# Storing only the rows that are needed, with an earlier band matrix and earlier transposes, in a convolution and spectral-mixing kernel

## The chip, the cores and the metric

The kernel runs on one core of one Trainium2 chip. The metric is device microseconds (us) of one execution. Most executions of one kernel agree within a few tenths of a per cent up to one per cent (the four fast ones of e17 took 190.2 to 190.98 us); a few fall into a slower state (193.1 and 194.22 us of e17) and are left out of the ratios. The experiments ran in four calls. Each call ran on one chip, together with runs of the kernel before, and the calls were on different chips; so a ratio holds within its call, and times of different calls compare less sharply.

## The reference

A causal convolution of 7 taps along the sequence, whose taps are softmax-normalised for each of 8 heads, then a spectral layer: the first 64 frequencies of the sequence are mixed over the 192 channels by complex matrices, transformed back and added, and a ReLU branch with a 192 x 192 matrix follows.

```python
batch, seq, d_model = (8, 3264, 192)        # n_heads 8, kernel_size 7, n_modes 64
w = softmax(weight, axis=-1)                # per head
x[b, s] = sum_k w[h, k] * x_pad[b, s + k]   # 6 zero rows ahead of the sequence
X = np.fft.rfft(x, axis=1)
Yr = Xr @ w_r - Xi @ w_i                    # for each of 64 modes, 192 x 192
Yi = Xr @ w_i + Xi @ w_r
y = np.fft.irfft(Y, n=S, axis=1)            # the other modes are zero
u = x + y
return u + np.maximum(u @ w_ch, 0.0)        # (8, 3264, 192), float32
```

## The kernel before

The sequence is cut into 27 windows of 122 rows (`WIN`), each held in the 128 partitions of the on-chip memory with 6 rows of overlap. The kernel first loads x and applies the convolution as a band matrix (`conv_unit`) and the forward transform. Then it streams 16 groups of mixing weights, and applies them one group at a time (`mix`). In the shadow of these mixes TensorE transposes the convolved x (`t_next`, one "pair" of chunks per call), because the last phase needs it that way. The last phase makes the output: 27 windows x 2 halves of the batch x 2 = 108 units, each ending in one VectorE add (of the sums in PSUM, where the kernel's matmuls leave them, and of x); two units fill one tile `t` of 128 partitions x 4 images x 192 values, and one store sends it off.

The stores and their order:

```python
    def finish_unit(u, zp):
        ...
        add = nc.vector.tensor_tensor(out=t[:, 2 * k:2 * k + 2, :], in0=zp[...], in1=x_all[...], op=ALU.add)
        if k == 0:
            return
        if w == NWIN - 1:
            rows = ((0, 80), (80, LASTVALID))
        elif w % CH == CH - 1:
            rows = ((0, 112), (112, WIN))
        else:
            rows = ((0, P),)                # 128 rows: 6 wrong ones, put right by the next window's store
        for i, (r0, r1) in enumerate(rows):
            dst = bass.AP(tensor=out.tensor, offset=out.offset + (4 * h * S + WIN * w + r0) * D,
                          ap=[[D, r1 - r0], [S * D, B // 2], [1, D]])
            if i == 0:
                nc.sync.dma_start(out=dst, in_=t[r0:r1, :, :])
            else:
                rest.append((dst, t[r0:r1, :, :]))   # six small rests, issued by ScalarE at the very end

    CH = 9                                  # chains of nine windows, three side by side
    wq = [(h, st + CH * c) for st in range(CH) for c in range(3) for h in range(2)]
```

A window has 122 good rows, but 128 are stored. The six too many lie where the next window's first rows belong, so the next window's store has to come after this one: a chain. Three chains per half run side by side, so that no store waits: in the profile of the kernel before, SyncE's queue waits ahead of its stores for adds (51.1 us) and for weights, never for an earlier store.

The mixes and the transposes in their shadow:

```python
    for g in range(NGRP):                   # 16 groups
        ...
        m = mix(g)
        ...
        if g in (0, 1, 2):
            load_weights(g + 7, wp)
        elif 7 <= g and g + 3 < NGRP:
            load_weights(g + 3, wp)         # the load of group 10 needs the buffer of group 7
        if not last:
            for _ in range(1 if g < 7 else 2):
                t_next(2 if g < 6 else 3)
            ...
        mix_t(g, *m)
```

In the last phase TensorE works with two row tiles of 64 rows each (64\*128 on the page, where the convolution has 128\*128). A tiny instruction, here called a word, by another engine orders the two tiles where both write the same sums; before, GpSimd gives it (`word = nc.gpsimd.nop()`, 17 ns each in the trace).

## Time and profile before

| | before |
|---|---|
| median of the first runs | 193.16 us (193.13 to 196.17) |
| span in the profile | 191.2 us |
| first convolution matmul | 17.87 us |
| x landed | 61.94 us |
| mix 0 / mix 7 starts | 75.41 / 89.81 us |
| last weights landed | 112.63 us |
| first / fifth add starts | 120.01 / 122.35 us |
| last add ends / last store landed | 181.56 / 189.83 us |
| store packets of 768 B, mean / median / 90th percentile | 40 / 38 / 44 ns |

The table is read from the trace. One row of one image is 192 x 4 = 768 B and is one packet (the stores of SyncE are 27,008 packets of 768 B in the trace). The prediction below shows the views that carry it. This is the list of transfer issues on the page of the kernel before, with the kilobytes of each and the median us from issue to landing, and it shows that SyncE's stores are nearly all of one kind, 384 KB, which is 128 rows of 4 images (SPq is SyncE's queue):

```profile
out_dram<-t SPq DMA_DIRECT2D x48, 384.0 KB, 5.1
```

Windows of the kernel before: start:end, length, busy time and count of PE, PEld, DVE, ACT, POOL, granted clock, DMA share, GB/s. PE is TensorE, PEld its loading of weights, DVE VectorE, ACT ScalarE, POOL GpSimd and SP SyncE. The granted clock is the share of TensorE's full clock that it was given. The DMA share is the time that all packets took, over the time of the core's 16 DMA engines (which carry out the transfers); it can exceed 1.

```profile
4.00:6.00 2.00, 0.00 (x0) 0.00 (x0) 1.93 (x3) 0.00 (x0) 2.00 (x2) 1.00 0.77 73
6.00:8.00 2.00, 0.00 (x0) 0.00 (x0) 1.92 (x5) 0.25 (x1) 2.00 (x3) 1.00 1.60 191
8.00:10.00 2.00, 0.00 (x0) 0.00 (x0) 1.84 (x6) 0.85 (x3) 2.00 (x3) 1.00 1.59 188
```

### The profile page before, as it was taken

The numbers are of one execution on the slowest core, as the hardware profiler recorded it, in microseconds if no ns is written. First come the engines' busy times: TensorE is split into PE (matmuls) and PEld (weight loads), VectorE is DVE, ScalarE is ACT, GpSimd is POOL, SyncE is SP. The second block draws the span as 40 slices with busy tenths as digits, with TensorE's granted clock in tenths as the row PEclk, the third lists the DMA queues.
The fourth block names the chain that finished last, engine by engine and source line by source line (L and its number), as shares of the span: only waits on it lengthen the run. The fifth ranks groups of instructions, "written<-read, shape, count | busy, mean of one in ns | idle before, by whom it ended". The sixth has DMA issues, their size and how long they took to land.

```text
span 191.2 us, 5496 instructions
## 1 busy us (share of the span) xinstructions
PE 152.2 (80%) x2146; PEld 131.1 (69%) x2146; DVE 128.5 (67%) x251; ACT 120.5 (63%) x217; POOL 49.5 (26%) x76
## 2 busy tenths in 40 slices
PE   0046657988997996999898889999999999999700
PEld 0002336777986874888686767999999999999500
DVE  7995742635334344466967735899999999999900
ACT  2196694454572662576686636888888888888500
POOL 8994334332523941520453100000000000000000
PEclk9999955899999998799999999999999999999985
DMA  1999999999999999999899920499999999999995
GB/s 18 171 191 191 192 192 192 192 193 192 194 191 193 194 202 208 206 206 184 122 194 196 202 38 2 141 318 318 323 324 318 322 322 322 319 326 324 309 276 157
DMA packets 65450, 41.47 MB, mean 217 GB/s; under 512 B 29968, under 2 KB 65424, under 8 KB 65424
## 3 DMA queue, kind: packets, MB, share of 16 engines
q0 software_dynamic: 37088, 20.14, 76.9%
q1 hardware_dynamic: 28016, 20.77, 35.6%
q8 instruction: 17, 0.28, 0.5%
q10 hardware_dynamic: 320, 0.20, 0.5%
q14 instruction: 9, 0.07, 0.1%
HBM read 40.31 MB, written 20.94 MB: 320 GB/s over the span
## 4 chain that ended last, share of the span: by engine, by line
DMA 35%; PE 28%; DVE 22%; POOL 6%; issue 2%; ACT 1%; DVEq 0%; POOLq 0%; ACTq 0%
DMA x_all<-in_x_dram 26%; DVE t L503 17%; PE z L451 9%; DMA wt<-in_moe_w_r_dram 9%; PE tp L361 7%; PE z L469 6%; POOL x_all L61 4%; PE yp L394 3%; DVE tail L322 2%; DVE cTa L365 2%; PE zwps L417 1%; PE z L441 1%; PE yp L404 1%; DVE cTb L365 1%; POOL wt L225 1%
## 5 line engine op out<-in xcount | busy, mean ns | idle before, releaser
L503 DVE TENSOR_TENSOR t<-z,x_all 128x384 f32<-128x384 f32 x108 | 59.8, 557 | 3.7 <-PE z L469 1.9
L474 ACT ACTIVATE z<-z 128x384 f32<-128x384 f32 x108 | 51.0, 475 | 10.5 <-ACT z L474 0.3
L469 PE MATMUL z<-zw,gst 64*128 64x384 bf16 x216 | 47.2, 323 | 0.2
L451 PE MATMUL z<-zw,gst 64*128 64x384 bf16 x216 | 46.7, 323 | 0.0
L451 PE MATMUL z<-win,cTa 64*128 64x192 bf16 x390 | 44.4, 243 | 0.0
L244 ACT CAST x_all<-cp 122x768 bf16<-122x768 f32 (+2 forms) x32 | 26.9, 878 | 22.7 <-PE cp L237 22.7
L451 PEld LDWEIGHTS <-cTa 64*128 64x128 bf16 x468 | 36.7, 94 | 1.8
L237 PE MATMUL cp<-x_all,cband 128*128 128x240 bf16 (+2 forms) x192 | 26.5, 279 | 8.4 <-DVE x_all L232 3.2
L246 DVE CAST x_all<-cp 122x960 bf16<-122x960 f32 (+2 forms) x16 | 17.0, 1063 | 21.5 <-PE cp L237 21.4
L237 PEld LDWEIGHTS <-cband 128*128 128x128 bf16 x192 | 18.8, 105 | 14.9 <-issue 8.4
L61 POOL DMA_DIRECT2D x_all<-in_x_dram x24 | 23.7, 1002 | 18.3 <-DMA x_all<-in_x_dram 18.3
L257 PE MATMUL xp<-x_all,fst 122*128 122x192 bf16 (+1 forms) x216 | 22.9, 255 | 0.9 <-DVE x_all L246 0.5
L257 PEld LDWEIGHTS <-fst 122*128 122x128 bf16 (+1 forms) x216 | 18.9, 102 | 2.2 <-DVE x_all L246 0.7
L451 PEld LDWEIGHTS <-gst 64*128 64x128 bf16 x216 | 19.9, 94 | 0.7 <-issue 0.2
L367 ACT COPY cTa<-tp 128x854 bf16<-128x854 bf16 (+1 forms) x16 | 14.5, 909 | 8.1 <-PE tp L361 8.1
L469 PEld LDWEIGHTS <-gst 64*128 64x128 bf16 x216 | 18.7, 94 | 1.0 <-POOLq L486 0.9
L451 PE MATMUL z<-win,cTb 64*128 64x192 bf16 x130 | 19.1, 243 | 0.0
L451 PE MATMUL z<-wB,cTa 64*128 64x192 bf16 x78 | 18.9, 243 | 0.0
L225 POOL DMA_DIRECT2D wt<-in_moe_w_r_dram x16 | 9.9, 618 | 28.3 <-PE yp L394 22.8
L365 DVE COPY cTa<-tp 128x854 bf16<-128x854 bf16 (+1 forms) x17 | 10.6, 625 | 8.5 <-PE tp L361 8.3
L176 PE MATMUL bps<-scaled,ident 128*128 128x512 bf16 x7 | 4.1, 585 | 14.0 <-ACT scaled L174 14.0
L361 PE MATMUL tp<-ident,x_all 122*128 122x122 bf16 x216 | 15.0, 224 | 0.0
(90 smaller groups left out, 181.4 us busy)
## 6 DMA issues: line engine op xcount, KB each, us to landing
out_dram<-t SPq DMA_DIRECT2D x48, 384.0 KB, 5.1
wt<-in_moe_w_r_dram POOLq DMA_DIRECT2D x16, 288.0 KB, 6.4
wt<-in_moe_w_i_dram POOLq DMA_DIRECT2D x16, 288.0 KB, 7.4
x_all<-in_x_dram POOLq DMA_DIRECT2D x8, 432.0 KB, 16.5
x_all<-in_x_dram POOLq DMA_DIRECT2D x9, 384.0 KB, 17.8
x_all<-in_x_dram POOLq DMA_DIRECT2D x7, 480.0 KB, 18.4
out_dram<-t SPq DMA_DIRECT2D x4, 336.0 KB
out_dram<-t SPq DMA_DIRECT2D x2, 240.0 KB, 4.4
```

Source lines behind the costliest of these rows:

```text
L61: nc.gpsimd.dma_start(out=x_all[:, b, c0:c0 + n, :], in_=src)
L237: nc.tensor.matmul(cp[:, j, 0:GRP * n].rearrange("p (w e) -> p w e", w=n), cband[:, h, :], x_all[:, b, w0:w0 + n, GRP * h:GRP * h + GRP], ...
L244: nc.scalar.copy(out=dst, in_=srcv)
L246: nc.vector.tensor_copy(out=dst, in_=srcv)
L257: nc.tensor.matmul(xp[:, 0:D], fst[0:k, c, :], x_all[0:k, b, c, :], start=(c == 0), stop=(c == NWIN - 1))
L361: nc.tensor.transpose(tp[:, WIN * k:WIN * k + WIN], slot_lhsT(p, k0 + k), ident[0:WIN, 0:WIN])
L365: nc.vector.tensor_copy(out=dst, in_=tp[:, 0:WIN * n])
L367: nc.scalar.copy(out=dst, in_=tp[:, 0:WIN * n])
L451: return nc.tensor.matmul(o, lhsT, rhs, start=start, stop=stop, skip_group_check=True, tile_position=(lo, 0))
L469: return [lambda: nc.tensor.matmul(zp[:, 0:2 * D], gst[lo:hi, WIN * w:WIN * w + P], zwi[(h, 1, k)][lo:hi, :], start=False, stop=(r == 1), ...
L474: return nc.scalar.activation(out=zp[:, 0:2 * D], in_=zp[:, 0:2 * D], func=ACT.Relu)
L503: add = nc.vector.tensor_tensor(out=t[:, 2 * k:2 * k + 2, :], in0=zp[:, 0:2 * D].rearrange("p (i e) -> p i e", i=2), in1=x_all[:, 4 * h + ...
```

## The change

The intent was to shorten both transfer phases. Stores send exactly the 122 good rows, as 112 rows by SyncE and 10 by GpSimd, so no bytes are sent twice, no chains are needed and no rests are left for the end. The band matrix is built packed (8 heads x 38 columns), so that the convolution starts earlier. The transposes are brought forward (two pairs in each of the first eight mixes). The first four units run on the whole array. ScalarE gives the words instead of GpSimd. The first large load is issued ahead of other setup work.

```diff
-        if w == NWIN - 1:
-            rows = ((0, 80), (80, LASTVALID))
-        elif w % CH == CH - 1:
-            rows = ((0, 112), (112, WIN))
-        else:
-            rows = ((0, P),)
-        for i, (r0, r1) in enumerate(rows):
-            dst = ...
-            if i == 0:
-                nc.sync.dma_start(out=dst, in_=t[r0:r1, :, :])
-            else:
-                rest.append((dst, t[r0:r1, :, :]))
+        r1, r2 = (80, LASTVALID) if w == NWIN - 1 else (112, WIN)
+        for q, ra, rb in ((nc.sync, 0, r1), (nc.gpsimd, r1, r2)):
+            dst = bass.AP(tensor=out.tensor, offset=out.offset + (4 * h * S + WIN * w + ra) * D,
+                          ap=[[D, rb - ra], [S * D, B // 2], [1, D]])
+            q.dma_start(out=dst, in_=t[ra:rb, :, :])
-    CH = 9
-    wq = [(h, st + CH * c) for st in range(CH) for c in range(3) for h in range(2)]
+    wq = [(0, worder[0])]                    # windows in their natural order, the halves one apart
+    for i in range(1, NWIN):
+        wq.append((0, worder[i]))
+        wq.append((1, worder[i - 1]))
+    wq.append((1, worder[-1]))
@@ transposes
-            for _ in range(1 if g < 7 else 2):
+            for _ in range(2 if g < 8 else 1):
@@ words of order
-                    word = nc.gpsimd.nop()
+        word = nc.scalar.nop()               # and one word a step instead of two
@@ band matrix: 28 ScalarE scalings and 7 predicated copies become
+        nc.vector.scalar_tensor_tensor(out=scaled[:, k, :, :], in0=diagc[...], scalar=float(k),
+                                       in1=wsb[...], op0=ALU.is_equal, op1=ALU.mult)   # 7 times
+        for o in bps:
+            nc.tensor.matmul(o[:, 0:H * NB], ident[:], scaled[...], start=(k == 0), stop=(k == KK - 1))
@@ first units
+    zw_part(0, 0, "va"); zw_part(0, 1, "vv")
+    for n in range(2): g_full(seq[n], zps[n], 0); relu(zps[n])     # whole array, no row tiles
+    ...
@@ cut: order of the loads, sine tables by unit, evictions, end of the rests
```

## The prediction

> **What bounds the kernel now.** I read the 40 slices first, then the windows, then who waited for whom, then the issuing queues. The slices:
>
> ```profile
> PE   0046657988997996999898889999999999999700
> PEld 0002336777986874888686767999999999999500
> DVE  7995742635334344466967735899999999999900
> ...
> DMA  1999999999999999999899920499999999999995
> GB/s 18 171 191 191 192 192 192 192 193 192 194 191 193 194 202 208 206 206 184 122 194 196 202 38 2 141 318 318 323 324 318 322 322 322 319 326 324 309 276 157
> ```
>
> A slice is 4.78 us. There are two transfer phases, with a hole between them. From about 5 to 111 us the load queue runs at 191 to 208 GB/s (x, then 16 groups of expert weights); from 122 to 189 us the stores run at about 320. So three things can shorten the program: an earlier or denser load phase, a smaller hole, a shorter store phase. The work of the engines inside a full transfer phase counts only through these. The windows show where each phase is loose:
>
> ```profile
> 86.00:90.00 4.00, 3.73 (x77) 3.16 (x78) 2.77 (x8) 2.48 (x5) 0.00 (x0) 1.00 1.20 205
> 90.00:91.00 1.00, 1.00 (x26) 0.91 (x23) 0.29 (x3) 1.00 (x2) 0.34 (x1) 1.00 0.44 73
> 91.00:92.00 1.00, 0.99 (x19) 0.87 (x17) 0.92 (x2) 0.71 (x2) 0.87 (x2) 1.00 0.22 22
> 92.00:93.00 1.00, 1.00 (x24) 0.80 (x22) 1.00 (x4) 0.95 (x3) 0.00 (x0) 1.00 0.68 46
> 93.00:94.00 1.00, 0.67 (x12) 0.45 (x9) 0.92 (x4) 0.59 (x3) 0.93 (x2) 1.00 1.12 185
> ...
> 110.00:111.00 1.00, 0.92 (x17) 0.71 (x14) 1.00 (x4) 0.63 (x2) 0.00 (x0) 1.00 0.82 144
> 111.00:112.00 1.00, 1.00 (x16) 0.87 (x13) 0.56 (x2) 0.75 (x1) 0.00 (x0) 1.00 0.15 21
> ```
>
> The last two columns are DMA share and GB/s. The load phase has one leak, some 2.5 us from 90.3 to 93, and its data ends at 111.1. The leak has a cause in the waits and in the timeline of GpSimd:
>
> ```profile
> POOL wt L225 <- PE yp L394: 22.8, 9, 7.8
> ...
> 82.24 0.63 POOL L225 DMA_DIRECT2D wt<-in_moe_w_i_dram  x1
> 90.66 0.61 POOL L225 DMA_DIRECT2D wt<-in_moe_w_r_dram  x1 [7.78 <-PE yp L394]
> ```
>
> Weight group 10 needs the buffer of group 7, so its load is issued only after mix 7 (89.8 to 90.4). Mix 0 itself starts at 75.4, although its weights were there long before (the first group was issued at 57.7, and a half group lands in a median of 6.4 to 7.4 us): the conv stage runs late, because the band matrix is only ready at about 18 us.
>
> The hole: the first add of the store phase starts at 120.0, the first store at 121.2. Then:
>
> ```profile
> L503 DVE TENSOR_TENSOR t<-z,x_all x108: 545/557/559, 120.0 to 181.0; 128x384 f32<-128x384 f32 x108
> L519 SPq DMA_DIRECT2D out_dram<-t x54: 372/1124/1728, 121.2 to 185.8; - x54
> ...
> 138.00:175.00 37.00, 37.00 (x649) 36.03 (x645) 35.95 (x65) 30.60 (x66) 0.00 (x0) 1.00 1.04 322
> 181.00:190.00 9.00, 0.00 (x0) 0.00 (x0) 0.56 (x2) 0.00 (x0) 0.00 (x0) 0.70 0.89 245
> ```
>
> The adds come every 0.572 us (61 us / 107), so a store is due every 1.144 us. A store issue took 372 ns at first and a median of 1124 ns later: SyncE is held back by full DMA engines. One store is 128 x 4 rows of 768 B = 393,216 B, and at 322 GB/s that is 1.22 us. The stores fall behind by 0.08 us each, and the last window shows the debt: adds end at 181.6, but the program at 191.2.
>
> [...] SyncE alone drives the engines to a share of 1.04[...]. [...] The raw order of ScalarE agrees (a 17 ns semaphore step begins inside a 475 ns ACTIVATE), so a ScalarE nop should not wait for the relu before it.
>
> **The change, part by part.**
>
> Start of loads. The first large load moves ahead of the iotas and of two small loads: from 2.67 us to about 0.9. The two small loads then take about 0.2 us inside the stream. Gain about 1.6 us on everything up to the end of x, since the stream is full.
>
> Packed band. The 28 ScalarE scalings (9.15 to 17.4) and 7 predicated copies are replaced by 7 VectorE products of 8x38 columns (about 0.4 us each, estimated at 304 columns and the rate of the 384-column add) and 14 matmuls. Band ready at about 10 us, the conv can start at about 11 (when the window-0 rows have landed) instead of 17.9. The sine work (4.3 us of ScalarE, 7.4 of VectorE) now lies between the first four units, which gives back perhaps 2 us. Conv units ran every 2.2 us or less and x arrives every 2.3, so the conv catches up with x (its chain ends at 61.9 before, so at 60.3 now). From the last conv unit to mix 0 took 4.4 us (70.95 to 75.4); with 1 us of lag that puts mix 0 at about 66 instead of 75.4.
>
> Early transposes. Mixes 0 to 7 now carry two transpose pairs each. With two pairs a mix took on average 2.8 us before (groups 8 to 14), with one about 2.05. So mix 7 ends at about 66 + 7 x 2.75 + 2.5 (g_parts and itself) = 88; before 90.4. The 9.4 us won at mix 0 shrink to 2.4 here. Load 10 is issued at 88.3; its data flow some 2.6 us later (before: 90.66 to 93.2), at about 91, while the shifted stream would run dry at about 89 (90.3 - 1.6): the leak shrinks to 2 us or less, it does not vanish. After that mixes carry one pair, the prefetch keeps up, and 12 half groups at 1.43 us (590 KB a group at 206 GB/s) end the landing at about 91 + 17.2 + receipt = 108.7. Before, it was 112.6. **Gain 3.9 us.**
>
> First units on the whole array. Before, from the last weights to the first add 7.4 us. Now: mix, transpose, yeT copy (2.3 as before), one zw part and its evictions, g_full, relu, g_full: first add at about +5.2. But the next units pass through the row-tiled pipeline, six steps deep, which starts after them: unit 4's add at about +10.7, with VectorE idle some 2 us. Adds end at +10.7 + 104 x 0.572 = +70.2; before +68.9. So this part alone **costs about 1.3 us** at the adds, though it starts the stores sooner.
>
> Exact rows. 54 stores of 122 x 4 rows: 488 rows instead of 512, 30.5 a DMA engine instead of 32, so 1.22 x 30.5/32 = 1.166 us a store against 1.144 us of adds. The debt grows by 0.02 us a store instead of 0.08: about 1.2 us instead of 4.2, and the last stores no longer wait for chains and six small ScalarE stores (179.5 to 188). End after the last add: 0.4 issue, some 2.3 latency, 1.7 debt and own transfer, 1.35 of the closing barrier = 5.8; before 191.2 - 181.6 = 9.6. **Gain 3.8 us.**
>
> ScalarE words. Per step one word instead of two[...]: PE needs it 0.5 us later. 0 us.
>
> Sum: 3.9 - 1.3 + 3.8 = 6.4 us: 193.16 - 6.4 = **186.8 us**.
>
> **Rivals.** (a) The ScalarE word waits for the relu. From the relu's start 0.71 us into a step plus 0.475, it would come 0.1 to 0.2 us after PE wants it, once a step; the step would grow from 0.572 to about 0.66 and the time by up to 9 us, to about 195. For it: program order; against: the semaphore step seen inside an ACTIVATE. (b) GpSimd's 54 small stores become the bound or disturb the engines: an issue of 10 rows took 0.55 us before and 1.144 are there, so the issue fits; but if 40 small rows hit the same engines[...] and the debt returns: 189 to 190 us. (c) The loads are full in any case, and mix 7 comes no earlier, as transposes are brought forward: the load phase gains only the 1.6 us of the start: about 189. (d) The other way, the leak closes wholly and PE's pipeline fills without a gap: 183.
>
> **Range and chances.** The parts are nearly independent, each good to 1 to 2 us, so 183.0 to 190.5. 2% faster is 189.3: (b) and (c) would have to come together, or (a) come true, to miss it. Faster 0.83, same 0.14, slower 0.03.
>
> **What would show it.** Band: first conv at about 11 us. Mix 0 at 64 to 68, mix 7 ended at 87 to 89.5, last weight landing 107 to 110. First add about 5 us after that, then a VectorE gap of 1 to 3 us at the fifth add. Adds every 0.57 us; if 0.65, rival (a). SyncE issues below 1.1 us; DMA at 315 to 322 GB/s to the end; last add to end 5 to 7 us. The prediction is wrong if the add period grows, if the leak stays 2.5 us or more, or if the small stores land last by microseconds.

What no trace or run of this case shows is cut out of the prediction and of three expectations, with the cuts marked. The sum came to 3.9 - 1.3 + 3.8 = 6.4 us, with 0 us for the words. The 0 us rests on the order in the trace alone: on ScalarE a 17 ns semaphore step begins at 122.141 us, 7 ns into an ACTIVATE of 475 ns that began at 122.134. The 30.5 or 32 rows for each of the 16 DMA engines are the author's estimate, 488 or 512 rows spread evenly. Three other figures can be read from the trace before: 2.3 us from issue to landing for the 3.8 KB load of x, 1.37 us from the last store's landing (189.83) to the end (191.2), and, for the receipt, 0.47 us from the end of the last packet of the weights' queue (112.16) to the landing of the last weights (112.63). That full DMA engines hold SyncE back is the author's reading; e11 agrees with it, where the adds set the pace and SyncE's issues took a median of 317 ns, against 1124 here.

## The result, and the profile after

The changed kernel took 205.28 us (median of 4 runs, 204.08 to 207.21, the last slow) against 193.83 us of the kernel before. The ratio is 1.058, with a 95% interval of 1.048 to 1.068. A ratio here is the mean time of one kernel's fast runs over the mean of the other's in the same rounds, so it is not quite the ratio of the medians quoted. The prediction of 186.8 us was 18.5 us too low and had the wrong sign; it had given slower a chance of 0.03.

| | before | after | predicted |
|---|---|---|---|
| first convolution matmul | 17.87 | 13.74 | about 11 |
| x landed | 61.94 | 63.08 | 60.3 |
| mix 0 starts | 75.41 | 67.66 | 66 |
| mix 7 starts | 89.81 | 90.13 | ends at 88 |
| last weights landed | 112.63 | 112.82 | 108.7 |
| first add, after last weights | +7.38 | +4.66 | +5.2 |
| fifth add, after last weights | +9.72 | +9.49 | +10.7 |
| last add ends | 181.56 | 191.74 | about 179 |
| last store landed | 189.83 | 201.24 | |
| store packets of 768 B, mean / median / 90th percentile, ns | 40 / 38 / 44 | 43 / 36 / 65 | 38.2 |

The slices of the page after (5.06 us each; the rows are as before):

```profile
DVE  5868964434434376767343277999866676686700
...
GB/s 47 162 189 192 192 194 191 192 193 191 192 189 142 205 204 207 206 206 143 175 200 200 10 78 167 257 237 279 246 251 265 235 282 245 256 259 259 247 264 179
```

From the 26th slice on, where the kernel before wrote at 318 to 326 GB/s with VectorE nearly always busy, this one writes at 235 to 282, and VectorE, after three slices in which it fills its free buffers, is only six to eight tenths busy. The windows over the leak, the steady store phase and the end (columns as above):

```profile
91.00:92.00 1.00, 0.50 (x10) 0.33 (x7) 0.83 (x2) 0.54 (x2) 1.00 (x2) 1.00 0.53 89
92.00:93.00 1.00, 0.65 (x10) 0.51 (x11) 0.88 (x3) 0.41 (x1) 0.17 (x1) 1.00 0.66 44
...
138.00:175.00 37.00, 31.95 (x524) 25.83 (x520) 26.39 (x52) 25.23 (x54) 14.20 (x27) 1.00 0.95 256
...
190.00:201.00 11.00, 0.11 (x1) 0.00 (x0) 1.74 (x4) 0.00 (x0) 1.28 (x3) 0.69 0.90 246
```

The window 138 to 175 is the core of the result: 322 GB/s before, 256 after, at a DMA share of 0.95 (before 1.04). The engines of the transfers are nearly as busy, and they get less done. Tile `t` in the trace after (durations min/median/max in ns, then first and last start; below, what VectorE and GpSimd waited for before working on `t`, us and times):

```profile
L532 DVE TENSOR_TENSOR t<-z,x_all x108: 547/558/559, 117.5 to 191.2; 128x384 f32<-128x384 f32 x108
L542 SPq DMA_DIRECT2D out_dram<-t x54: 317/1275/2390, 118.6 to 197.5; - x54
L542 POOL DMA_DIRECT2D out_dram<-t x54: 545/545/602, 119.2 to 192.0; - x54
...
  DVE t L532: 43.9, 53
  DVE zw L452: 13.1, 1
  DMA out_dram<-t: 10.2, 10
```

An add still takes 558 ns (557 before), and a GpSimd issue of ten rows 545 to 602 ns (552 before, for a load), so neither is seen to disturb the other. What is new is the last line: VectorE waits 10.2 us for stores to give their buffers back, which it never did before. The stores pace the adds. In the load phase, GpSimd's timeline shows that the load of weight group 10 is issued no earlier than before (90.66):

```profile
90.96 0.61 POOL L234 DMA_DIRECT2D wt<-in_moe_w_r_dram  x1 [8.62 <-PE yp L418]
```

And VectorE's timeline at the start of the store phase has the gap before the fifth add that the prediction expected, 1.84 us:

```profile
119.46 1.01 DVE L532 TENSOR_TENSOR t<-z,x_all 128x384 f32<-128x384 f32 x2
122.31 1.70 DVE L532 TENSOR_TENSOR t<-z,x_all 128x384 f32<-128x384 f32 x3 [1.84 <-PE z L497]
```

A store's mean period in that window is 122 x 4 x 768 = 374,784 B over 256 GB/s, 1.464 us. The prediction had 1.166. Over 54 stores that is 16.1 us, nearly the whole miss.

### The profile page after: what moved, and what is told of

Its sections match the earlier page's. It is cut to its first block, busy times and chain, and to the rows that moved or that the text cites. A ratio compares the mean times of both kernels' runs of the same rounds, so it can differ in the third digit from the quotient of the medians.

```text
span 202.2 us, 5511 instructions
## 1 busy us (share of the span) xinstructions
PE 154.9 (77%) x2145; PEld 128.7 (64%) x2145; DVE 123.3 (61%) x257; ACT 114.3 (57%) x197; POOL 79.1 (39%) x131
## 4 chain that ended last, share of the span: by engine, by line
DMA 52%; PE 19%; DVE 14%; issue 4%; POOL 3%; ACT 2%; POOLq 0%; DVEq 0%; ACTq 0%
DMA x_all<-in_x_dram 28%; DMA out_dram<-t 16%; DVE t L532 10%; DMA wt<-in_moe_w_i_dram 7%; PE tp L385 6%; PE z L480 5%; PE yp L418 3%; PE z L497 2%; DVE cTa L389 2%; DVE tail L346 2%; POOL x_all L61 1%; ACT cTa L391 1%; ACT z L502 1%; PE zwps L441 1%; POOL wt L234 1%
## 5 line engine op out<-in xcount | busy, mean ns | idle before, releaser
L532 DVE TENSOR_TENSOR t<-z,x_all 128x384 f32<-128x384 f32 x108 | 56.7, 555 | 17.1 <-DMA out_dram<-t 10.2
L542 POOL DMA_DIRECT2D out_dram<-t x54 | 29.5, 547 | 57.0 <-DVE t L532 43.9
L480 PE MATMUL z<-zw,gst 64*128 64x384 bf16 x208 | 41.1, 323 | 6.9 <-DVE t L532 6.8
L480 PE MATMUL z<-win,cTa 64*128 64x192 bf16 x385 | 41.5, 243 | 0.0
L497 PE MATMUL z<-zw,gst 64*128 64x384 bf16 x208 | 41.1, 323 | 0.2
L250 ACT CAST x_all<-cp 122x768 bf16<-122x768 f32 (+2 forms) x34 | 28.4, 873 | 19.7 <-PE cp L243 19.7
L480 PEld LDWEIGHTS <-cTa 64*128 64x128 bf16 x462 | 32.4, 94 | 4.3
L243 PE MATMUL cp<-x_all,cband 128*128 128x240 bf16 (+2 forms) x192 | 25.1, 280 | 9.8 <-DMA x_all<-in_x_dram 4.9
L480 PEld LDWEIGHTS <-gst 64*128 64x128 bf16 x208 | 17.3, 94 | 11.2 <-issue 10.9
L252 DVE CAST x_all<-cp 122x960 bf16<-122x960 f32 (+2 forms) x14 | 15.0, 1072 | 15.0 <-PE cp L243 14.9
L389 DVE COPY cTa<-tp 128x854 bf16<-128x854 bf16 (+1 forms) x17 | 10.6, 625 | 8.2 <-PE tp L385 7.9
L480 PEld LDWEIGHTS <-cTb 64*128 64x128 bf16 x162 | 14.4, 94 | 1.8
```

What stands on the lines that cost most here:

```text
L243: nc.tensor.matmul(cp[:, j, 0:GRP * n].rearrange("p (w e) -> p w e", w=n), cband[:, h, :], x_all[:, b, w0:w0 + n, GRP * h:GRP * h + GRP], ...
L250: nc.scalar.copy(out=dst, in_=srcv)
L252: nc.vector.tensor_copy(out=dst, in_=srcv)
L480: return nc.tensor.matmul(o, lhsT, rhs, start=start, stop=stop, skip_group_check=True, tile_position=(lo, 0))
L497: return [lambda: nc.tensor.matmul(zp[:, 0:2 * D], gst[lo:hi, WIN * w:WIN * w + P], zwi[(h, 1, k)][lo:hi, :], start=False, stop=(r == 1), ...
L542: q.dma_start(out=dst, in_=t[ra:rb, :, :])
```

## The experiments

Fourteen kernels ran. The first theory was that two queues, SyncE's and GpSimd's, disturb each other on the same DMA engines (theory A in the expectations, which tell their theories by letters). Its rivals: the exact rows or the new order are at fault, whoever issues them (B), neighbouring windows written at nearly the same time collide (C), GpSimd's path is itself slow for stores (D), the 112-row stores themselves are slow, perhaps only because 7 rows an engine (112 / 16, if they spread evenly) is an odd number (E), and the missing chains let stores run together in a bad way (F).

### e1_sync10: one queue

```diff
-        for q, ra, rb in ((nc.sync, 0, r1), (nc.gpsimd, r1, r2)):
+        for q, ra, rb in ((nc.sync, 0, r1), (nc.sync, r1, r2)):
```

> The changed kernel with its 10-row stores issued by SyncE too, nothing else changed. In the changed kernel the stores ran at some 255 GB/s (before: 322). Theory A, the small GpSimd stores slow the DMA engines down by mixing a second queue into them: with one queue the rate returns to 305 GB/s or more [...], the store phase falls from 80 to about 67 us and the time from 205 to 190-193 us. Theory B, the exact rows or the new order of windows are the cause, whoever issues them: the rate stays at 250-265 GB/s and the time at 202-206 us.

Measured: 201.66 us (201.35 to 202.78), ratio to before 1.041 (1.037 to 1.046); 257 GB/s from 138 to 175 us, against 256 for the changed kernel. Its 768-B packets took 44 ns in the mean, 36 in the median, 67 at the 90th percentile. One queue does not bring the rate back, so theory A falls. Of the profiled runs e1 took 2.7 us less than the changed kernel (201.35 against 204.08 us), but its last weights had landed 2.9 us earlier, so none of the loss need belong to the second queue.

### e2_no10: without the ten rows (wrong)

```diff
-        for q, ra, rb in ((nc.sync, 0, r1), (nc.gpsimd, r1, r2)):
+        for q, ra, rb in ((nc.sync, 0, r1),):
```

> The changed kernel without its 10-row stores: the result is wrong on purpose (10 rows of each window are never written). It shows the 112-row stores and the new order alone. Theory A (mixing): 448 rows a store, 28 an engine, about 1.07 us, less than the 1.144 us of two adds, so no debt at all: adds every 0.572 us to the end, DMA near 300 GB/s because the adds limit it, time 186-189 us. Theory B (shape or order): the engines stay the limit, below 265 GB/s, store phase over 70 us, time 196 us or more.

Measured: 193.19 us (one run), between what the two theories expected. The window of that trace:

```profile
138.00:175.00 37.00, 37.00 (x652) 34.47 (x648) 35.76 (x65) 30.76 (x65) 0.00 (x0) 1.00 0.99 279
```

A store of 112 rows is 344,064 B, at 279 GB/s 1.233 us. Its packets took 44 ns, as in e1, and 28 packets for each DMA engine (112 x 4 / 16, if they spread evenly, an estimate) x 44 ns is 1.232 us. The ten-row store of the changed kernel then costs 1.464 - 1.233 = 0.23 us, although it has only 8% of the bytes. It costs the same when SyncE issues it: in e1 the period is 374,784 B over 257 GB/s, 1.458 us. So 112 rows alone are already as slow as 128 rows were before (1.22 us), and the ten come on top.

### e3_oldorder: the order of the windows

The changed kernel with the unit order of before:

```diff
-    wq = [(0, worder[0])] ...
+    wq = [(h, st + 9 * c) for st in range(9) for c in range(3) for h in range(2)]
```

> The changed kernel with the order of units of before (three chains nine windows apart, both halves in turn), exact rows and 10-row GpSimd stores kept. Theory C, writing neighbouring windows one after another is what slows the writes: the rate returns to over 305 GB/s and the time to about 190 us. Theory A: no change, 250-260 GB/s and 203-207 us.

Measured: 207.51 us (one run), 255 GB/s from 138 to 175 us. Writing windows far apart does not help; theory C falls.

### e4_allpool: one store of 122 rows by GpSimd

```diff
-        for q, ra, rb in ((nc.sync, 0, r1), (nc.gpsimd, r1, r2)):
+        for q, ra, rb in ((nc.gpsimd, 0, r2),):
```

> The changed kernel with one 122-row store a window pair, issued by GpSimd; SyncE stores nothing. One queue only, but the software one, whose 3072-byte packets in the changed kernel took a median of 122 ns against four times 36-38 ns for SyncE's rows of 768 B. Theory A (mixing of two queues): at least 305 GB/s, time 186-192 us; if the large packets are really cheaper, the adds limit (no debt) and it is 186-188. Theory D, GpSimd's path itself is slow for stores: below 265 GB/s, time over 203 us.

Measured: 424.78 us, ratio 2.19. The trace holds 29,480 packets of 24 B in the store phase and others of 4,608 B, and the tile's view shows the cost:

```profile
L542 POOL DMA_DIRECT2D out_dram<-t x54: 1281/2452/2491, 119.0 to 406.6; - x54
...
  DMA out_dram<-t: 205.0, 42
```

GpSimd's issue takes 2.45 us, and VectorE waits 205 us for buffers. An exact store in one piece from this queue is no way out.

### e8_oldstores: everything but the stores

The changed kernel with the stores, chains, order and ScalarE rests of before:

```diff
+            rows = ((0, 80), (80, LASTVALID)) / ((0, 112), (112, WIN)) / ((0, P),)   # as before
+    wq = [(h, st + CH * c) for st in range(CH) for c in range(3) for h in range(2)]
+    for dst, src in rest: nc.scalar.dma_start(out=dst, in_=src)
```

> The changed kernel with the stores of before (128 rows, chains of nine windows, the last ten rows by ScalarE) and their order of units; all else of the change stays. Theory E, the 112-row stores are what is slow: the rate returns to 315-324 GB/s, SyncE issues near 1.12 us, and what is left is the rest of the change: 188-192 us. If another part of the change slows the engines in the store phase (the ScalarE words, the pipeline), the rate stays under 270 GB/s and the time over 200 us.

Measured: 194.7 us (193.34 to 195.39), ratio 1.004 (0.998 to 1.011). The rate is back:

```profile
138.00:175.00 37.00, 37.00 (x652) 34.51 (x648) 36.04 (x66) 30.69 (x65) 0.00 (x0) 1.00 1.04 320
```

Two things follow. The stores are the whole loss (205.28 - 194.7 = 10.6 us). And the rest of the change, for which 3.9 - 1.3 = 2.6 us had been predicted, is worth nothing here: mix 7 starts at 89.40 and the last weights land at 112.04.

### e9_before_exact: the stores alone

The kernel before, with 112 + 10 rows by SyncE and nothing else changed:

```diff
-        if w == NWIN - 1: ... else: rows = ((0, P),)
+        r1, r2 = (80, LASTVALID) if w == NWIN - 1 else (112, WIN)
+        for ra, rb in ((0, r1), (r1, r2)):
+            nc.sync.dma_start(out=..., in_=t[ra:rb, :, :])
```

> The kernel before with only its stores changed: 112 and 10 rows, exact, both by SyncE, no chains, order of units as before. Theory E: the stores alone bring the loss: 255-262 GB/s, store phase about 80 us, time 203-207 us. If the loss needs another part of the change: over 300 GB/s and 190-195 us.

Measured: 205.62 us (203.98 to 206.03), ratio 1.058 (1.051 to 1.065), and the rate of the changed kernel:

```profile
138.00:175.00 37.00, 33.08 (x542) 26.98 (x539) 28.02 (x55) 25.64 (x55) 0.00 (x0) 1.00 0.94 259
```

The stores alone bring the loss, on either front.

### e10_128free and e11_96rows: rows without chains (both wrong)

e10 stores 128 rows at distances of 128, so nothing overlaps and nothing is chained, with as many bytes in all as exact rows have. e11 stores only rows 0 to 95 of each window.

```diff
 e10
-        for q, ra, rb in ((nc.sync, 0, r1), (nc.gpsimd, r1, r2)):
-            dst = ... (4 * h * S + WIN * w + ra) * D ...
+        dst = ... (4 * h * S + 128 * w) * D ...            # 26 windows, the last of 64 rows
+        nc.sync.dma_start(out=dst, in_=t[0:n, :, :])
 e11
+        r1, r2 = (80, LASTVALID) if w == NWIN - 1 else (96, WIN)
+        for q, ra, rb in ((nc.sync, 0, r1),):
```

> The changed kernel with 128-row stores of SyncE that neither overlap nor wait for each other (window w goes to row 128 w, the last window is not stored: a wrong result on purpose). Theory E (the number of rows decides): 318-324 GB/s and about 38-40 ns a row, as with the chains of before. Theory F (without chains too many stores are in flight and the engines lose time): below 270 GB/s and 43 ns a row or more.

> The changed kernel with stores of rows 0 to 96 by SyncE only (a wrong result on purpose). 384 rows a store, 24 an engine. Theory E [...]: 43-45 ns a row as with 112, but 24 x 44 = 1.06 us a store is under the 1.144 us of the adds, so no debt and adds every 0.572 us. In its form that odd counts (7) are bad and even ones (6) are not: 38-40 ns.

Measured, e10: 188.81 us (one run), packets of 40 / 39 / 42 ns. Its window:

```profile
138.00:175.00 37.00, 37.00 (x651) 34.43 (x647) 35.77 (x65) 30.67 (x65) 0.00 (x0) 1.00 1.04 320
```

Measured, e11: 188.43 us (one run), packets of 44 / 36 / 66 ns. Its window:

```profile
138.00:175.00 37.00, 37.00 (x652) 34.55 (x648) 36.03 (x66) 30.76 (x65) 0.00 (x0) 1.00 0.94 260
```

The chains are innocent (F falls): free stores of 128 rows have the good packets. With 96 rows the adds, not the transfers, set the pace (294,912 B every 1.144 us is 258 GB/s), so its rate says nothing, but its packets do: they are as dear as at 112 rows. It is the number of rows, not the distance of 122 (the kernel before has it, with good packets), nor an odd count for each engine (96 rows give 6, if they spread evenly), nor the ten, that makes packets dear.

### e12_pairs, e13_front, e14_best: what the other parts are worth

e12 is e8 with the transposes laid out otherwise. e13 has the changed kernel's front (loads, band, first stages) and everything else from before. e14 is e13 with e12's transposes, ScalarE's words, and the six small rests sent by GpSimd at once.

```diff
 e12 (against e8)
-            for _ in range(2 if g < 8 else 1):
+            for _ in range(1 if g < 6 else 2):
 e14 (against e13)
-            for _ in range(1 if g < 7 else 2):
+            for _ in range(1 if g < 6 else 2):
-                    word = nc.gpsimd.nop()
+                    word = nc.scalar.nop()
-                rest.append((dst, t[r0:r1, :, :]))
+                nc.gpsimd.dma_start(out=dst, in_=t[r0:r1, :, :])
```

> The changed kernel with the stores of before (as in e8_oldstores) and the transposes of the weights laid out one pair per frequency unit for units 0 to 5 and two pairs from unit 6, instead of two pairs for units 0 to 7. Theory: two pairs for every one of the first eight mixes make a mix cost some 3.0 to 3.4 us instead of 2.75, so that mix 7 ends no earlier than before (89.4 us in e8) and the last two loads of spectra still wait for their buffers; with one pair early on, mix 7 ends near 86.3, the wait before the tenth load closes, the last weights land at 109 to 110 us (112.04 in e8), the fifth unit's first sum comes near 120 us (122.80 in e8) and the time is 190 to 191 us (194.7 in e8). Rival: the pairs are not what paces the mixes (the loads are); then mix 7 stays at 89 or later, weights at 112 and the time at 194 to 195.

> The changed kernel's front alone (order of the loads, packed band, first stages) with everything of the kernel before from the mixes on: its transposes, its words of order by GpSimd, its first units on half the array, its stores. If the packed band alone is worth what the prediction gave it: mix 0 near 67 us, mix 7 near 86.5 us, the last weights at 110, the first sum 7.4 us later (117.4), the last sum near 179 us, landed near 187, time near 190 us. Rival: the mixes come no faster than the loads let them, mix 7 near 89, and the time is that of before, 193 to 194.

> Meant as the best version: the front of e13, the transposes of e12 (one pair for units 0 to 5, then two), ScalarE's words of order, the 128-row chained stores of before by SyncE and the six small rests issued by GpSimd as soon as they are ready. If the parts add: 188 to 189 us, mix 7 near 86.3, last weights 109 to 110. If the transposes are not what paces: 192 to 194 us, as e8_oldstores.

| | time, us | ratio to before (95%) | mix 0 | mix 7 | last weights | first add | last add | landed |
|---|---|---|---|---|---|---|---|---|
| e8_oldstores | 194.7 | 1.004 (0.998 to 1.011) | 66.86 | 89.40 | 112.04 | 116.86 | 182.06 | 190.04 |
| e12_pairs | 192.36 | 0.991 (0.982 to 1.000) | 66.75 | 86.61 | 110.72 | 116.16 | 181.14 | 190.50 |
| e13_front | 191.9 | 0.989 (0.980 to 0.997) | 65.75 | 86.28 | 109.59 | 117.59 | 178.85 | 187.43 |
| e14_best | 193.95 | 0.996 (0.986 to 1.006) | 66.70 | 87.20 | 112.94 | 119.92 | 181.83 | 191.88 |

The time of e12 lies 1.4 us above its expectation, e13 at 1.9 us above; e14 missed by 5 us and is the worst of the three. In e12 the fifth add, expected near 120 us, came at 122.10. Against e8, mix 7 came 2.8 us earlier in e12 (86.61 against 89.40). Its timeline of GpSimd, and its list of waits (us, times, longest):

```profile
87.44 0.61 POOL L234 DMA_DIRECT2D wt<-in_moe_w_r_dram  x1 [5.79 <-PE yp L418]
```

```profile
PE yp L418 <- DMA wt<-in_moe_w_i_dram: 7.0, 9, 1.3
```

Load 10 is issued 3.5 us earlier than in the changed kernel, and the mixes wait for the load stream nine times. From mix 0 to mix 7 a mix came every 2.84 us in e12, which is one group of 590 KB at 206 GB/s (2.86 us). With two pairs it was 22.47 / 7 = 3.21 us in the changed kernel.

But the layout of the transposes is not the whole of that difference, and e12 does not settle it. Ten of the profiled kernels have the changed front and two pairs in each early mix. From mix 1 to mix 7 they all took 18.50 to 18.54 us, 3.09 us a mix, against 17.28 in e12: some 1.2 us come with the second pair. From mix 0 to mix 1, however, five of the ten took 2.6 to 2.7 us (2.58 in e12) and the other five 3.9 to 4.0. In four of these five TensorE's granted clock was 0.5 just then (from 67.8 to 71.3 us in the changed kernel, whose 32 transposes took 3.29 us instead of 2.00 in e8); in e8 mix 1 waited 1.46 us for its weights. So e1, with two pairs, has mix 7 at 86.80, load 10 at 87.63 and the last weights at 109.95, as good as e12. Over the ten the last weights landed at 109.95 to 113.78 us, 111.7 in the mean; with one pair (e12, e13, e14) at 109.59 to 112.94. The second pair is slower by 0.2 us a mix; that it decides when the weights land is not shown.

Why e14 lost is only partly settled. After its last add it needed 10.05 us to land, where e13 needed 8.58; its 64 packets of 3,072 B from GpSimd took 444 ns in the mean, beside SyncE's. But its weights also landed 3.3 us later than e13's in the profiled run, for which I have no test.

### e15_64x2 and e16_128x2: partitions or pieces (both wrong)

e15 and e16 are e10 with each 128-row store cut in two: e15 into partitions 0 to 63 and 64 to 127, e16 into images 0, 1 and images 2, 3, so that both halves keep 128 partitions. The bytes, their places and the number of issues are the same.

```diff
 e15
-        nc.sync.dma_start(out=dst, in_=t[0:n, :, :])
+        for r0 in range(0, n, 64):
+            nc.sync.dma_start(out=dst, in_=t[r0:r0 + 64, :, :])        # dst 64 rows further on
 e16
+        for b0 in (0, 2):
+            nc.sync.dma_start(out=dst, in_=t[0:n, b0:b0 + 2, :])       # dst two images further on
```

> Wrong on purpose, as e10_128free: 128-row stores at whole distances, without overlap or chains, but each one cut into two stores of 64 rows (partitions 0 to 63 and 64 to 127), both by SyncE. The same bytes go to the same places as in e10 (40 ns a row, 310 to 322 GB/s). Theory that what counts is how the rows of one transfer fall on the 16 DMA engines [...]: rows of 43 ns and over, the 90th percentile at 60 ns or more, under 300 GB/s, as at 112 and 96 rows. Rival, that only an odd number of rows per engine or the volume counts: 40 ns and 315 GB/s as in e10, unless SyncE's issue (two for each unit) becomes the bound, which its issue time in the trace will tell.

> Wrong on purpose, as e10_128free: the 128-row stores at whole distances, each cut into two stores by images (images 0 and 1, then 2 and 3 of the half), so that each has all 128 rows (partitions) and half of the bytes; SyncE issues twice as many, as in e15_64x2. If the number of rows of a transfer decides: packets of 40 ns with a 90th percentile near 42, 310 to 322 GB/s from 130 us on, about 188 to 190 us. Rival, the size or the number of transfers, or SyncE's issue: as in e15_64x2, 45 ns, 220 to 246 GB/s, 207 to 209 us.

The same window of e15, and then of e16:

```profile
138.00:175.00 37.00, 29.86 (x472) 22.49 (x469) 23.25 (x47) 22.63 (x48) 0.00 (x0) 1.00 0.88 245
```

```profile
138.00:175.00 37.00, 35.94 (x625) 32.83 (x621) 33.95 (x63) 29.50 (x63) 0.00 (x0) 1.00 0.99 304
```

Measured: e15 208.77 us, e16 191.27 us (one run each). Packets: 45 / 36 / 66 ns in e15, 40 / 38 / 45 in e16. That is the cleanest pair: the same bytes in as many pieces of the same size, and only the cut across partitions makes packets dear. Smaller pieces as such cost a little (304 against e10's 320 GB/s). Dear packets are only part of the lost rate: 304 x 40 / 45 would be some 270 GB/s (an estimate), and the engines were also less busy, at a share of 0.88 against 0.99. The expectation named SyncE's issue as a rival for that. In the traces an issue took at least 595 ns in e15 (median 696) and 372 in e16 (457). Two of them, at least 1.19 us, fit in the 1.6 us that e15 took for a tile (393,216 B over 245 GB/s), so the issue alone does not set the pace; how much of the idle time it causes is not settled.

### e17_words: ScalarE's words alone

e13 with `word = nc.scalar.nop()` in place of `nc.gpsimd.nop()`.

> e13_front with one edit: the word of order between the row tiles by ScalarE instead of GpSimd. The prediction gave it 0 us in the store phase: the sums stay 0.572 us apart and the time within the noise of e13_front, 191 to 193 us. Rival (a) of the prediction, that the words wait behind ScalarE's own relus: sums further apart than 0.58 us while stores' buffers are free, and 194 us or more.

Measured: 190.83 us (190.2 to 194.22; two of six runs, the profiled one among them, slow), ratio of fast runs 0.979 (0.972 to 0.987). The four fast runs took 190.2 to 190.98. The words cost nothing; whether they gain against e13 (0.980 to 0.997, on another chip) is not settled, since the intervals overlap. It has the lowest ratio of the correct versions, 2% below the kernel before and, by the two ratios (0.979 / 1.058 = 0.926), 7% below the changed one.

## Why the prediction was wrong, point by point

**Exact rows: this step failed.** It took the cost of a row from the 128-row stores (38.2 ns) and scaled by rows, 30.5 a DMA engine if they spread evenly. The mis-sized term is the cost of a row, and it is mis-sized in two parts. The 112 rows: 28 packets x 44 ns = 1.23 us instead of 28 x 38.2 = 1.07, so 0.16 us a store. The ten rows: 0.23 us (e2) instead of 2.5 x 38.2 ns = 0.10, so 0.13 us a store. Together 0.29 us x 54 = 16 us. The 3.8 us of gain became a loss of 10.6 us (after against e8); stores alone lost 11.8 us on the kernel before (205.62 - 193.83, e9).

Why ten rows cost so much is not shown: the trace does not tell a packet's engine, and the even spread of their 40 packets, 2.5 to each, was the author's estimate. In the changed kernel they went as packets of 3,072 B, ten for each store, at 281 ns in the mean where four rows of 38.2 would be 153; as SyncE's ten rows of 768-B packets cost as much (e1, a period of 1.458 us against 1.464), that form is not the reason.

Why fewer rows make packets dear is not shown either. The prediction had the cost of a row at 128 rows alone; that it would hold at 112 was assumed. e15 against e16 gives the direction: 245 against 304 GB/s, from the same bytes. With fewer than 128 rows the median packet takes 36 ns, below the 38 of before, but the 90th percentile is 65 to 67 ns (after, e1, e11, e15) against 42 to 45 at 128 rows (before, e10, e16), and the mean 43 to 45 against 40. Stores of 112 + 10 rows ran at 255 to 259 GB/s from 138 to 175 us, whole ones of 128 rows at 320 to 322 (before, e8, e10). That the number of rows of a store decides what its packets cost is shown (e10, e11, e15, e16); the cause is not.

**The rival (b)** was the nearest: it named the small stores. It made them worth 2 to 3 us. What it lacked was the dearer row: it still counted 38.2 ns, and e1, with no GpSimd in the stores, lost 4.1%.

**Early transposes: failed; in this trace rival (c) held.** The mis-sized term is the period of a mix. 2.75 us with two pairs was taken from the late groups; that is less than one group of weights takes at the rate of the loads (2.86 us). Measured were 22.47 us from mix 0 to mix 7, 3.2 us more than 7 x 2.75: 2.0 from the steady 3.09 us of mixes 1 to 7, found in all ten kernels with this layout, and 1.2 from the first step, in which TensorE's granted clock was 0.50. So mix 7 came at 90.13, the leak stayed (89 and 44 GB/s from 91 to 93 us), and the last weights landed at 112.82 instead of 108.7. In the other runs with this layout they landed at 109.95 to 113.78, never at 108.7. e13, with one pair, is 1% below before (0.980 to 0.997); e12 reaches from 0.982 to 1.000. One pair early may be the better layout, but the traces do not show it (see e12).

**Packed band: right in kind.** The first convolution came 2.7 us later than predicted (13.74), but mix 0, at 67.66, was 7.75 us earlier than before.

**Start of loads: not gained.** These are the windows of the changed kernel that answer to those of before above:

```profile
4.00:6.00 2.00, 0.00 (x0) 0.11 (x1) 1.52 (x9) 0.25 (x1) 2.00 (x4) 1.00 1.53 181
6.00:8.00 2.00, 1.45 (x6) 0.84 (x6) 1.98 (x6) 0.00 (x0) 2.00 (x4) 1.00 1.32 145
8.00:10.00 2.00, 2.00 (x9) 1.03 (x7) 1.54 (x4) 0.00 (x0) 2.00 (x3) 1.00 1.46 165
```

Data flows earlier (181 against 73 GB/s), but from 6 to 10 us it then flows at 145 and 165 instead of 191 and 188, just while VectorE makes the packed band. x landed at 63.08, later than before. I did not test the cause: the profiled runs of kernels with the same front had x between 61.11 (e1) and 63.71 us (e3), so part of it varies from run to run.

**First units on the whole array: the gap came as said, the cost is open.** First add 4.66 us after the last weights (predicted 5.2), VectorE idle 1.84 us (some 2), but the fifth add at +9.49 where before it was at +9.72. So in this trace nothing was lost, and nothing won. In e8 and e12, with the same first units, the fifth add came 10.76 and 11.38 us after the last weights, so the cost stays open.

**ScalarE's words: right,** 0 us. In e8 and e14 the adds come 0.57 us apart (from the fifth add to the end of the last, (182.06 - 122.80) / 104 and (181.83 - 122.19) / 104), as before, and rival (a) falls.

**GpSimd's issue: right.** The prediction counted 0.55 us for ten rows; its issues took 545 to 602 ns throughout.

One sum of the prediction is off by little: 61 us / 107 is 0.570 us, not 0.572, which makes 0.2 us over 104 adds.

As a sum: everything but the stores was to bring -2.6 us and brought +0.9 (e8 against before, 194.7 and 193.83), a miss of 3.5; the stores were to bring -3.8 and brought +10.6, a miss of 14.4. Together that is 17.9 of the 18.5 us.

## What to carry to other kernels

Before trimming the rows of a transfer that covers all 128 partitions, measure the trimmed shape: here 122 rows instead of 128, 5% fewer bytes, cut into 112 + 10, cost 20% of the rate (256 against 322 GB/s), and six redundant rows were the cheaper choice. If a store has to be cut, try first to cut along the free dimensions and keep all partitions (304 against 245 GB/s here). Before reading a difference of one trace as the effect of an edit, look how far the same stage varies in the traces that share its code: here mix 7 started anywhere from 86.80 to 90.84 us. Before moving work into a stage that is paced by loads, compare its period with the bytes of one load over the load rate (here 3.09 us a mix with two pairs, against 2.86 us a group of weights).
